# Five grad V stores of a decode attention backward, issued by GpSimd in pieces that leave out one DMA engine

## The chip, the cores and the metric

One core of one Trainium2 chip. The metric is the device time of one execution in microseconds (us). The engines are named as in the profile: PE (TensorE) does matmuls, PEld is its weight load, DVE is VectorE, ACT is ScalarE, POOL is GpSimd, SP is SyncE. ACT, SP and POOL can issue DMAs; the transfers themselves are done by 16 DMA engines that the core has.

## The reference

Attention with one query row per head, forward and backward. B, H, Sq, Sk, D = 2, 32, 1, 8192, 128, all in bfloat16, so there are 64 heads, each with a K and a V of 8192 x 128 (2 MB each).

```python
def _fwd_reference(q, k, v):
    scale = q.shape[-1] ** -0.5
    scores = jnp.einsum("bhqd,bhkd->bhqk", q, k) * scale
    p = _softmax(scores, axis=-1)
    return jnp.einsum("bhqk,bhkd->bhqd", p, v)
...
    _out, _vjp = jax.vjp(_f, q, k, v)
    _grads = _vjp(grad_out)
```

The outputs are the attention output, grad q (both 64 x 128), grad K and grad V (64 x 8192 x 128 each). In one head, with weights p: dp = V grad_out; ds = p (dp - sum(p dp)) scale; grad V is the outer product of p and grad_out, grad K that of ds and q. Some 268 MB are read and 268 MB written.

## The kernel before

A head's K lies in SBUF as 128 partitions of 64 rows of 128 numbers, 16 KB on each partition; V likewise. Five such pairs of buffers (kt, vt; UNITS = 5) are used in turn. K and V are loaded whole, one DMA each on SP's queue (load, L103). PE transposes 128 x 128 blocks with an identity (L112), ACT copies most of them and DVE a few from PSUM to bfloat16 (L119, L117), PE multiplies the transposed blocks with the columns of q and grad_out (L135), which gives scores and dp. Softmax runs on DVE and ACT (L159 to L227). PE then adds up the weighted rows for the output and grad q (L240). DVE writes the outer products over the inputs: grad V into the buffer of V, grad K into the buffer of K (outer, L270, in four quarters each), and `store` (L278) sends the buffer to HBM as one DMA of 128 x 16 KB on ACT's queue. The last head's stores go in halves.

The order is written out by hand. The loop runs over h; iteration h computes scores and dp of head h and finishes head p = h - 1 (weighted rows, outer products, stores), in NS = 8 steps j. The store of grad V of p stands in step 4, that of grad K in step 7, and at the end of step 7 SP is given the loads of head h + 3, which take the buffers of head h - 2 and therefore wait until its two stores have landed:

```python
                if x and p < BH - 1 and j in (4, 7):
                    store(p, j // 7)
...
                    for i in ((), (0,), (1, 2), (3, 4), (5,), (6,), (7,), ())[j]:
                        outer_and_store(p, i // 4, i % 4)
...
                    if x and UNITS <= h + 3 < BH:
                        load(h + 3)
```

The DMAs of SP and ACT carry eight semaphores in turn, so a DMA also waits until the eighth one before it has landed; in an iteration there are two stores and two loads, so a store waits for the same store two heads before. GpSimd makes the identities and fills the zero blocks of wz at the start (L292) and does nothing afterwards.

Of the kernel before, what the change touches and what calls it, by code (L numbers as in the profile page):

```python
# [11 lines left out]
BF16 = mybir.dt.bfloat16  # L12
# [3 lines left out]
HC = CH // 2  # L16
QG = 4
OG = 4
UNITS = 5


@with_exitstack
def kernel(
# [11 lines left out]
    nc = tc.nc  # L35
# [6 lines left out]
    assert NT * P == Sk and NT == 4 * CH and BH <= P and BH % QG == 0  # L42
    assert BH % OG == 0 and OG * 8 == 32
    NS = 2 * NT // CH
    scale = float(D) ** -0.5

    const = ctx.enter_context(tc.tile_pool(name="const", bufs=1))
# [6 lines left out]

    pick = const.tile([P, 4, 2, OG], F32)
    idv = ident_f[:].rearrange("p (g w k j) -> p g j w k", g=4, w=2, k=OG)
    nc.vector.tensor_copy(out=pick[:], in_=idv[:, 0])
    for g in range(1, 4):
        nc.vector.tensor_add(out=pick[:], in0=pick[:], in1=idv[:, g])

    q_rows = q.rearrange("b h s d -> (b h s) d")
# [3 lines left out]

    kvp = ctx.enter_context(tc.tile_pool(name="kv", bufs=UNITS))
    evp = ctx.enter_context(tc.tile_pool(name="ev", bufs=5))
# [8 lines left out]
    dk_v = out_2.rearrange("b h (p n) d -> (b h) p n d", n=NT)  # L76
    dv_v = out_3.rearrange("b h (p n) d -> (b h) p n d", n=NT)
# [8 lines left out]
    wz = [  # L86
        [const.tile([P, NT // 4, 32], BF16, name=f"wz{w}{k}") for k in range(OG)]
        for w in range(2)
# [5 lines left out]
    heads = [Head() for _ in range(BH)]  # L94

    def load(h):
        x = heads[h]
        x.kv = [
            kvp.tile([P, NT, D], BF16, name="kt", tag="kt"),
            kvp.tile([P, NT, D], BF16, name="vt", tag="vt"),  # L100
        ]
        for dst, src in zip(x.kv, (k_v, v_v)):
            nc.sync.dma_start(out=dst[:], in_=src[h])  # L103

    def transposes(h, j, u):

        x = heads[h]
        w, c = divmod(j, NS // 2)
        tp = ps_tp.tile([P, HC, P], F32, name="tp", tag="tp")
        for i in range(HC):  # L110
            n = c * CH + u * HC + i
            nc.tensor.matmul(  # L112
                tp[:, i, :], lhsT=x.kv[w][:, n, :], rhs=ident_bf[:], start=True, stop=True
            )
        ev = evp.tile([P, HC, P], BF16, name="ev", tag="ev")
        if u and j in (0, 7):
            nc.vector.tensor_copy(out=ev[:], in_=tp[:])  # L117
        else:
            nc.scalar.copy(out=ev[:], in_=tp[:])  # L119
        x.ev = getattr(x, "ev", {})  # L120
        x.ev[j, u] = ev

    def products(h, j, u):
        x = heads[h]
        w, c = divmod(j, NS // 2)
        if c == 0 and u == 0:
            if w:
                x.dp = ps_one.tile([P, NT + 2], F32, name="dp", tag="dp")
            else:
                x.sm = ps_one.tile([P, NT + P + 1], F32, name="sm", tag="sm")  # L130
        ev = x.ev.pop((j, u))
        col = (qT_all, doT_all)[w][:, h : h + 1]
        for i in range(HC):
            n = c * CH + u * HC + i
            nc.tensor.matmul(  # L135
                (x.dp if w else x.sm)[:, n : n + 1], lhsT=ev[:, i, :], rhs=col,
                start=True, stop=True,
            )
# [22 lines left out]
    def all_max(x):  # L161
        mT = x.sm[0:1, NT : NT + P]
        nc.tensor.transpose(mT, x.mp[:], ident_f[:])  # L163
        x.gm = work.tile([1, 1], F32, name="gm", tag="gm")
        nc.vector.reduce_max(out=x.gm[:], in_=mT, axis=AX.X)

    def exps(x):
        mb = x.sm[:, NT + P : NT + P + 1]
        nc.tensor.matmul(mb, lhsT=ones_f[0:1, :], rhs=x.gm[:], start=True, stop=True)  # L169
        negm = work.tile([P, 1], F32, name="negm", tag="negm")  # L170
        nc.vector.tensor_scalar(out=negm[:], in0=mb, scalar1=-scale, scalar2=None, op0=ALU.mult)  # L171
        x.E = work.tile([P, NT], F32, name="E_f", tag="E_f")
        x.ld = work.tile([P, 2], F32, name="ld", tag="ld")
        nc.scalar.activation(  # L174
            out=x.E[:],
            in_=x.sm[:, 0:NT],
            func=ACT.Exp,
            bias=negm[:],
            scale=scale,
            accum_out=x.ld[:, 0:1],  # L180
        )

    def to_weights(h, w, src):
        k = h % OG
        nc.vector.tensor_copy(  # L185
            out=wz[w][k][:, :, 16 * w + 4 * k : 16 * w + 4 * k + 4],
            in_=src[:].rearrange("p (m j) -> p m j", j=4),
        )

    def deltas(x):  # L190
        junk = work.tile([P, NT], BF16, name="junk", tag="junk")
        nc.vector.tensor_tensor_reduce(  # L192
            out=junk[:],
            in0=x.E[:],
            in1=x.dp[:, 0:NT],
            scale=1.0,
            scalar=0.0,
            op0=ALU.mult,
            op1=ALU.add,
            accum_out=x.ld[:, 1:2],  # L200
        )

    def sums(x):
        x.lsum = x.dp[:, NT : NT + 2]
        nc.tensor.matmul(x.lsum, lhsT=ones_f[:], rhs=x.ld[:], start=True, stop=True)  # L205
# [27 lines left out]
    def weighted_rows(h, w, chunks):  # L233


        rows, k = heads[h].kv[1 - w], h % OG
        for c in chunks:
            for g in range(4):
                n = c * CH + 4 * g
                nc.tensor.matmul(  # L240
                    acc[32 * g : 32 * g + 32, :],
                    lhsT=wz[w][k][:, n // 4, :],
                    rhs=rows[:, n : n + 4, :].rearrange("p n d -> p (n d)"),
                    start=(w == 0 and k == 0 and c == 0),
                    stop=(w == 1 and k == OG - 1 and c == NT // CH - 1),
                    tile_position=(0, 32 * g),
                )
# [17 lines left out]
    def outer(h, w, i):  # L265
# [8 lines left out]
            op=ALU.mult,  # L274
        )

    def store(h, w, a=0, b=NT):
        nc.scalar.dma_start(out=(dv_v, dk_v)[w][h][:, a:b, :], in_=heads[h].kv[1 - w][:, a:b, :])  # L278

    def outer_and_store(h, w, i):  # L280
# [3 lines left out]
            store(h, w, (i - 1) * CH, (i + 1) * CH)  # L284


    nat = const.tile([BH, 2, D], BF16)
    for i, src in enumerate((q_rows, do_rows)):
        nc.scalar.dma_start(out=nat[:, i, :], in_=src)
# [8 lines left out]
    with tc.manual_schedule():  # L298
        for h in range(min(UNITS, BH)):
            load(h)  # L300
        for h in range(BH + 1):
            p = h - 1
            x = heads[p] if h else None
            y = heads[h] if h < BH else None
            full = h and p % OG == OG - 1
            for j in range(NS):
                for u in range(2):
                    if y:
                        transposes(h, j, u)
                    if u == 0:  # L310
                        if x and j == 1:
                            sums(x)
                        if y and j == 5:
                            all_max(y)
                        if y and j == 6:
                            exps(y)
                    if y and j:
                        products(h, j - 1, u)
                    elif x and j == 0:
                        products(p, NS - 1, u)  # L320
                    if x and j < 4:
                        weighted_rows(p, j // 2, (2 * (j % 2) + u,))
                if x and j == 0:
                    deltas(x)
                if x and j == 1:
                    weights(p)
                if y and j == 4:
                    row_max(y)
                if y and j == 7:
                    to_weights(h, 0, y.E)  # L330
                if x and p < BH - 1 and j in (4, 7):
                    store(p, j // 7)
                if x:
                    for i in ((), (0,), (1, 2), (3, 4), (5,), (6,), (7,), ())[j]:
                        outer_and_store(p, i // 4, i % 4)
                    if full and j == 4:
                        acc_to_sbuf(x)
                    if full and j == 6:
                        combine(p)
                if j == 7:  # L340
                    if x and UNITS <= h + 3 < BH:
                        load(h + 3)
                    if y and h % QG == 0:
                        spread_rows(h // QG)
        for w, dst in enumerate((o_rows, dq_rows)):
            tps = ps_tp.tile([BH, P], BF16, name="tps", tag="tp")
            nc.tensor.transpose(tps[:], colsT[:, w, :], ident_bf[:])
            rows = const.tile([BH, D], BF16, name=f"rows{w}")
            nc.scalar.copy(out=rows[:], in_=tps[:])
            nc.scalar.dma_start(out=dst, in_=rows[:])  # L350


# [28 lines left out]
```

## Time and profile before

| | |
|---|---|
| median of 3 runs | 1305.08 us (1302.08 to 1305.24) |
| the profiled execution | 1302.89 us, its span 1301.1 us |
| mean granted TensorE clock | 0.885 |
| PE, PEld, DVE, ACT, POOL busy | 1108.2, 911.0, 887.4, 906.3, 4.8 us (85, 70, 68, 70, 0%) |
| moved by DMA | 539.65 MB in 37653 packets, mean 415 GB/s |
| loads, SP queue: issue to landing | K 18.9 us, V 28.5 us (median of 64 each) |
| stores, ACT queue: issue to landing | grad V 38.2 us, grad K 40.3 us (median of 63 each) |
| the longest group | L119 ACT, 896 copies of 1025 ns, 879.8 us |

The span is from the first to the last instruction of the profiled execution; the rest of its time lies around it. A share counts busy time over the whole span. "To landing" runs from the issue of a DMA to the arrival of its last bytes, with all that it waits for behind other transfers. A packet is what a DMA engine moves as one piece; here nearly all are one partition's 16 KB. Queue q1 carries the loads, q10 the stores and the small transfers of ACT, q8 the fetches of instructions.

### The profile page before, as it was taken

How to read it: one execution, taken by the hardware profiler on the slowest of the kernel's cores; microseconds unless marked ns; L12 is line 12 of the kernel's file. 1: busy time of each engine (PE TensorE's matmuls, PEld its weight loads, DVE VectorE, ACT ScalarE, POOL GpSimd, SP SyncE). 2: the span in 40 equal slices, each digit the busy share in tenths (PEclk: the TensorE clock that was granted, in tenths of full speed). 3: DMA queues.
4: the chain of work that ended last, by engine and by line, in shares of the span. 5: the costliest groups of instructions: out<-in, count | busy, mean ns of one | idle time of the engine just before them, and what ended most of it. 6: DMA issues, size and time to landing. Idle time of an engine off the chain costs nothing.

```text
span 1301.1 us, 42243 instructions
## 1 busy us (share of the span) xinstructions
PE 1108.2 (85%) x18948; PEld 911.0 (70%) x18948; DVE 887.4 (68%) x1511; ACT 906.3 (70%) x1043; POOL 4.8 (0%) x16
## 2 busy tenths in 40 slices
PE   5999998988889879898898888988889888888784
PEld 5777777766767667677776767767767677677673
DVE  2887777766766767667676676766667667676566
ACT  5887778867767767676776766766668576676562
POOL 1000000000000000000000000000000000000000
PEclk9999989889887998888898888888899888898786
DMA  9999999999999999999999999999999999999986
GB/s 396 418 427 427 426 428 426 428 427 429 427 428 426 426 419 421 421 427 421 418 421 421 426 421 418 421 408 421 416 418 417 411 425 419 413 412 421 391 356 268
DMA packets 37653, 539.65 MB, mean 415 GB/s; under 512 B 4448, under 2 KB 4448, under 8 KB 4448
## 3 DMA queue, kind: packets, MB, share of 16 engines
q1 hardware_dynamic: 18432, 268.44, 49.6%
q10 hardware_dynamic: 19040, 268.51, 48.7%
q8 instruction: 148, 2.42, 0.7%
q14 instruction: 33, 0.27, 0.1%
HBM read 268.47 MB, written 268.47 MB: 413 GB/s over the span
## 4 chain that ended last, share of the span: by engine, by line
DMA 76%; PE 10%; ACT 6%; issue 4%; DVE 3%; ACTq 0%; DVEq 0%; SPq 0%
DMA out_dram<-kt 74%; PE tp L112 6%; ACT ev L119 5%; DVE ev L117 2%; PE acc L240 2%; DMA kt<-in_k_dram 1%; PE sm L135 1%; DMA nat<-in_grad_out_dram 1%; PE dp L205 0%; DVE kt L270 0%; DVE vt L270 0%; PE dp L135 0%; ACT E_f L174 0%; PE c L258 0%; PE sm L163 0%
## 5 line engine op out<-in xcount | busy, mean ns | idle before, releaser
L119 ACT CAST ev<-tp 128x1024 bf16<-128x1024 f32 x896 | 879.8, 1025 | 326.7 <-PE tp L112 270.7
L112 PE MATMUL tp<-ident_bf,kt 128*128 128x128 bf16 x4096 | 375.8, 245 | 83.3 <-DMA kt<-in_k_dram 54.8
L112 PEld LDWEIGHTS <-kt 128*128 128x128 bf16 x4096 | 281.1, 110 | 218.0 <-issue 156.4
L112 PE MATMUL tp<-ident_bf,vt 128*128 128x128 bf16 x4096 | 316.7, 221 | 60.4 <-ACT ev L119 44.3
L135 PEld LDWEIGHTS <-ev 128*128 128x128 bf16 x8192 | 332.4, 100 | 2.1 <-issue 0.2
L112 PEld LDWEIGHTS <-vt 128*128 128x128 bf16 x4096 | 260.9, 98 | 94.6 <-issue 74.2
L117 DVE CAST ev<-tp 128x1024 bf16<-128x1024 f32 x128 | 156.7, 1224 | 246.0 <-PE tp L112 237.3
L270 DVE TENSOR_TENSOR kt<-qd,dS 128x2048 bf16<-128x2048 bf16 x256 | 310.0, 1212 | 0.0
L270 DVE TENSOR_TENSOR vt<-qd,P 128x2048 bf16<-128x2048 bf16 x256 | 295.8, 1216 | 0.0
L135 PE MATMUL dp<-doT_all,ev 128*128 128x1 bf16 x4096 | 178.9, 165 | 0.1
L135 PE MATMUL sm<-qT_all,ev 128*128 128x1 bf16 x4096 | 178.6, 164 | 0.0
L240 PE MATMUL acc<-vt,wz 128*32 128x512 bf16 x1024 | 124.3, 476 | 9.3 <-DVE wz L185 9.2
L240 PE MATMUL acc<-kt,wz 128*32 128x512 bf16 x1024 | 108.2, 415 | 0.4 <-DVE wz L185 0.4
L240 PEld LDWEIGHTS <-wz 128*32 128x32 bf16 x2048 | 53.6, 95 | 21.7 <-DVE wz L185 12.4
L159 DVE TENSOR_REDUCE mp<-sm 128x1 f32<-128x64 f32 x64 | 14.4, 225 | 74.3 <-PE sm L135 74.3
L153 ACT CAST qd<-pb 128x1024 bf16<-128x1024 f32 x16 | 16.2, 1012 | 43.4 <-DMA out_dram<-kt 39.6
L210 DVE RECIPROCAL rl_all<-dp 128x1 f32<-128x1 f32 x64 | 10.8, 168 | 39.6 <-PE dp L205 39.6
L205 PE MATMUL dp<-ld,ones_f 128*128 128x2 f32 x128 | 28.4, 291 | 8.8 <-DVE ld L192 8.6
L205 PEld LDWEIGHTS dp<-ld,ones_f 128*128 128x128 f32 x128 | 24.8, 242 | 14.1 <-DVE ld L192 13.5
L171 DVE TENSOR_SCALAR negm<-sm 128x1 f32<-128x1 f32 x64 | 9.9, 154 | 23.9 <-PE sm L169 23.9
L169 PE MATMUL sm<-gm,ones_f 1*128 1x1 f32 x128 | 24.4, 257 | 0.0
L169 PEld LDWEIGHTS sm<-gm,ones_f 1*128 1x128 f32 x128 | 18.9, 184 | 6.7 <-issue 0.2
(40 smaller groups left out, 277.4 us busy)
## 6 DMA issues: line engine op xcount, KB each, us to landing
kt<-in_k_dram SPq DMA_DIRECT2D x64, 2048.0 KB, 18.9
vt<-in_v_dram SPq DMA_DIRECT2D x64, 2048.0 KB, 28.5
out_dram<-vt ACTq DMA_DIRECT2D x63, 2048.0 KB, 38.2
out_dram<-kt ACTq DMA_DIRECT2D x63, 2048.0 KB, 40.3
out_dram<-vt ACTq DMA_DIRECT2D x2, 1024.0 KB, 8.4
out_dram<-kt ACTq DMA_DIRECT2D x2, 1024.0 KB, 8.5
out_dram<-rows ACTq DMA_DIRECT2D x2, 16.0 KB, 7.4
nat<-in_q_dram ACTq DMA_DIRECT2D x1, 16.0 KB, 8.2
```

The lines of the kernel that those rows point to most:

```text
L112: nc.tensor.matmul(tp[:, i, :], lhsT=x.kv[w][:, n, :], rhs=ident_bf[:], start=True, stop=True)
L117: nc.vector.tensor_copy(out=ev[:], in_=tp[:])
L119: nc.scalar.copy(out=ev[:], in_=tp[:])
L135: nc.tensor.matmul((x.dp if w else x.sm)[:, n : n + 1], lhsT=ev[:, i, :], rhs=col, start=True, stop=True,)
L153: nc.scalar.copy(out=qd[:], in_=pb[:])
L159: nc.vector.reduce_max(out=x.mp[:], in_=x.sm[:, 0:NT], axis=AX.X)
L169: nc.tensor.matmul(mb, lhsT=ones_f[0:1, :], rhs=x.gm[:], start=True, stop=True)
L171: nc.vector.tensor_scalar(out=negm[:], in0=mb, scalar1=-scale, scalar2=None, op0=ALU.mult)
L205: nc.tensor.matmul(x.lsum, lhsT=ones_f[:], rhs=x.ld[:], start=True, stop=True)
L210: nc.vector.reciprocal(out=rl, in_=x.lsum[:, 0:1])
L240: nc.tensor.matmul(acc[32 * g : 32 * g + 32, :], lhsT=wz[w][k][:, n // 4, :], rhs=rows[:, n : n + 4, :].rearrange("p n d -> p (n d)"), sta ...
L270: nc.vector.tensor_tensor(out=x.kv[1 - w][:, n : n + CH, :].rearrange("p n (d t) -> p n d t", t=2), in0=row.unsqueeze(1).to_broadcast([P, ...
```

## The change

Where (2h + w) mod 26 is 12, that is for grad V (w = 0) of heads 6, 19, 32, 45 and 58, `store` no longer issues one DMA on ACT's queue but calls `store_by_fifteen`, which issues the same 128 partitions from GpSimd in 24 pieces: for each r of 0 to 3, eleven partitions from 52 + r in steps of 4, four from r, three from 20 + r, eight from 96 + r and four from 32 + r, and the pair 16 + r and 48 + r (`fifth`). These pairs are the eight partitions that the change ascribes to the fifth DMA engine. The pieces of four are given 16384 as the longest run (`max_dma_last_dim`), the others 8192. Between the pieces stand ten small transfers, `turn(n)`, which copy four numbers of each of n rows of q into a scratch tile (`spare`), each into columns of its own; they are there to move the turn in which GpSimd's DMAs are given to engines. One more `turn(5)` stands at the start, ahead of the fills of wz on GpSimd, and a `turn(11)` at the end: 5 x 34 + 2 = 172 DMAs from GpSimd in all.

```diff
+RARE = 26
...
+    turns = []
+
+    def turn(n):
+
+        i = 4 * len(turns)
+        turns.append(n)
+        two = lambda t: t.rearrange("p (a b) -> p a b", a=2)
+        nc.gpsimd.dma_start(
+            out=two(spare[0:n, :])[:, :, i : i + 2], in_=two(q_rows[0:n, :])[:, :, 0:2]
+        )
+
+    def store_by_fifteen(h, w):
...
+        dst, src = (dv_v, dk_v)[w][h], heads[h].kv[1 - w]
+
+        def rows(lo, n, step=4, size=8192):
+            own = slice(lo, lo + step * (n - 1) + 1, step)
+            nc.gpsimd.dma_start(out=dst[own], in_=src[own], max_dma_last_dim=size)
+
+        def fifth(r):
+            rows(16 + r, 2, step=32)
+
+        for r in range(4):
+
+            if r == 1:
+                fifth(r)
+                turn(14)
+            rows(52 + r, 11)
+            rows(r, 4, size=16384)
+            if r == 0:
+                fifth(r)
+                turn(3)
+            elif r == 3:
+                turn(10)
+                fifth(r)
+                turn(9)
+            else:
+                turn(5)
+            rows(20 + r, 3)
+            if r == 2:
+                fifth(r)
+                turn(14)
+            rows(96 + r, 8)
+            rows(32 + r, 4, size=16384)
+            turn(5)
+
     def store(h, w, a=0, b=NT):
+        if (2 * h + w) % RARE == RARE // 2 - 1:
+            return store_by_fifteen(h, w)
         nc.scalar.dma_start(out=(dv_v, dk_v)[w][h][:, a:b, :], in_=heads[h].kv[1 - w][:, a:b, :])
...
+    spare = const.tile([16, 1024], BF16)
+    turn(5)
     nat = const.tile([BH, 2, D], BF16)
...
             nc.scalar.dma_start(out=dst, in_=rows[:])
+        turn(11)
```

## The prediction

> **What bounds the kernel now.** I read the page's strip and DMA parts first, then its chain, then the chain in order of time, then stretches of the span, and last the packet records behind them.
>
> The page:
>
> ```profile
> DMA  9999999999999999999999999999999999999986
> GB/s 396 418 427 427 426 428 426 428 427 429 427 428 426 426 419 421 421 427 421 418 421 421 426 421 418 421 408 421 416 418 417 411 425 419 413 412 421 391 356 268
> ...
> q1 hardware_dynamic: 18432, 268.44, 49.6%
> q10 hardware_dynamic: 19040, 268.51, 48.7%
> q8 instruction: 148, 2.42, 0.7%
> ...
> DMA 76%; PE 10%; ACT 6%; issue 4%; DVE 3%; ACTq 0%; DVEq 0%; SPq 0%
> ```
>
> The DMA engines are never idle, yet what they move sinks from 427 to some 415 GB/s: something takes longer per byte late in the run, with no engine seen idle. The chain is DMA. In order of time it repeats every four heads (columns: start, length, what):
>
> ```profile
> 1011.59 40.25 DMA out_dram<-kt
> 1051.90 37.05 DMA out_dram<-kt
> 1088.96 3.42 issue
> 1092.37 40.41 DMA out_dram<-kt
> 1132.85 36.71 DMA out_dram<-kt
> 1169.56 3.70 issue
> ```
>
> 40.4 + 36.7 + 3.7 = 80.8 us for four heads, 20.2 a head: a K store lands and lets the K store two heads later be issued (its semaphore is the one of eight DMAs before), and the loads into its buffer. SyncE shows the same; its waits in all:
>
> ```profile
> SPq L103 <- DMA out_dram<-kt: 1143.0, 59, 40.5
> ```
>
> Stretches of the span (busy us of PE, PEld, DVE, ACT and POOL, clock, DMA share, GB/s):
>
> ```profile
> 100.00:300.00 200.00, 180.37 (x3232) 148.37 (x3231) 150.29 (x257) 154.16 (x178) 0.00 (x0) 0.94 1.01 427
> 900.00:1100.00 200.00, 172.61 (x2935) 141.43 (x2934) 136.53 (x234) 139.91 (x162) 0.00 (x0) 0.88 1.00 417
> ...
> 1229.50:1233.00 3.50, 0.00 (x0) 0.00 (x0) 0.47 (x1) 0.00 (x0) 0.00 (x0) 1.00 0.35 150
> ...
> 1265.00:1272.50 7.50, 7.22 (x144) 5.92 (x141) 7.23 (x12) 6.54 (x7) 0.00 (x0) 1.00 0.11 42
> ```
>
> A DMA share of 0.11 is below two engines of 16, so in the tail nearly all others wait for one. To see whether that one is late all along, I followed the engines through the trace's packet records (start, length, queue, bytes). A 16 KB packet takes 611 ns and the next on its engine starts 4 ns before it ends; each 2 MB transfer gives every engine eight packets and a 4-byte one that counts it done. With these two rules the records fall into 16 rows up to 1139 us of the span:
> - One engine (the laggard) has packets of median 628 ns and up to 685; it finishes 1.580 packets per us throughout (1738 in 1100 us).
> - Eight engines have 611 ns packets and a gap of some 0.9 us about every 70 us, as long as the fetches on q8 (median 949 ns; 148 / 8 = 18.5 each): 1.612 per us before they are held back.
> - Seven have 611 ns and no such gaps: 1.64.
>
> So the laggard falls behind: by 4 packets at 139 us, 15 at 439, 26 at 839, and then no more, since the others wait for it. Late stores land on it 27 us after the others (store of V 47: others at 974, it at 1001). Each engine has the equal of 2048 packets: 65 are done at 39 us of the span, so the laggard needs 39 + 1983 / 1.580 = 1294 us, and the last large store ends at 1295 (some 6 us of small stores follow). The whole run is the length of this one engine's work. The profiled execution took 1302.89 (span 1301.1 and 1.8 around it), 2.2 below the median 1305.08 of the three runs; these took no profile and are as long, so the lag is no work of the profiler.
>
> **The change, part by part.**
>
> *Eight rows taken off one engine, five times.* 5 x 8 = 40 packets at 1 / 1.580 us are 25.3 us of the laggard's time, if the fifth engine is the laggard. It then ends at 39 + (2008 - 65) / 1.580 = 1269 of the span instead of 1294. The rows go one each to eight others: 5 x 0.61 = 3.1 us each. The fetch engines become its equals: 39 + 1983 / 1.612 = 1269, or 1272 for one that gets five rows more; the seven fast ones end at 1251. So the work bound falls by 22 to 25 us. A head costs 32 / 1.612 = 19.85 us against 20.2, or 422 GB/s against 414.
>
> *The tail.* It holds 13.5 us in which 15 engines wait: 3.5 at 1229.5, 7.5 at 1265, 2.5 at 1282.5. The first two are mostly the laggard (V of the last head lands on it at about 1261, on the others about 1255); the last is VectorE's products before the final stores. Balanced, some 5 us of idle time remain for every engine, where the laggard now has nearly none. That is given back: 1269 to 1272, plus 5, is 1274 to 1277 for the last large store, 18 to 21 us sooner.
>
> *Can compute follow at 19.85 us?* Up to 300 us it ran ahead: V stores 5, 8 and 11 are issued 54.7 and 51.7 us apart, 17.2 to 18.2 a head. PE has 1108 / 64 = 17.3 us of work a head. Yes, with some 1.5 us to spare.
>
> *34 DMAs on GpSimd in place of one on ScalarE* (24 pieces, 10 small transfers), five times, 172 with the two at the ends. GpSimd works only in the first 5.4 us, so nothing queues behind them but the eight fills of wz at the start, first needed after the first loads. The one before them on the queue is the first small transfer. What counts is when all 24 pieces have landed, since the V buffer waits for that. No row shows a DMA issued by GpSimd. Lower bound: 0.34 us each, as one on ScalarE's queue: 34 x 0.34 = 12 us. Upper bound: each waits for the one before to land, and the shortest landing of a store is 7.0: 34 x 7.0 = 238 us. With waits eight back, as the loads and stores have them, it is 34 / 8 x 7.0 = 30 us and a last landing, 37. I take 37, as these rows are the nearest. The whole store takes 38.2 today. The Trainium skill (DMA: Bandwidth & Descriptors, § Specifications) gives about 1 us to the first byte of a DMA from GpSimd; one after the other, 34 would be some 34 us, an estimate, and the sum would stay as it is. The same skill (SBUF — State Buffer, § SBUF: two separate sides) warns that VectorE instructions in a two-port mode keep GpSimd from writing descriptors, which speaks against this change; no row here shows it.
>
> What covers 37 us: the K store of the same head lands 10 us after the V store, and SyncE asks for the K buffer first, so 48 us cost nothing. Beyond, the load queue runs dry, but four stores in flight are 32 packets, 19 us more of work. So up to some 68 us the engines stay busy; beyond, each us is lost. ScalarE's next stores meet their old semaphores earlier or as now, since one DMA fewer lies between.
>
> *Packets.* An 8 KB packet takes 309 ns (the last stores' row), twice that is 7 ns over 611: 16 to 18 on an engine, 0.1 us a store. Small transfers: some 150 runs of 4 bytes, 9 an engine, between 9 ns (the counting packet) and 18 (a 256-byte one): 0.2 us. 34 counting packets on each engine: 34 x 6 to 9 ns = 0.3 us. Together 0.6 us a store, 3 us in all. Below nothing is excluded: it is work added.
>
> *Sum:* 1302.9 - 20 + 3 = 1286; on the median 1305.1 - 17 = 1288. I say 1287.
>
> **Rivals.**
> - *The laggard isn't the fifth engine, or the pieces fall on other engines than meant.* The trace gives packets no engine number, so nothing in it says which of the 16 is late. The laggard keeps its 1294 us, and at worst takes five more rows (3 us) and the 3 us of small packets: 1303 to 1309, no change. Chance 0.10. The Trainium skill (DMA: Bandwidth & Descriptors, § Latency and other measured facts) has engines 7 and 15 as the usually slower ones, and by that the change would unload the wrong engine; the trace disagrees so far, with one slow engine and not two. The skill also says (same page, § Why a DMA increments its semaphore by 16 and not by 1) that a DMA from GpSimd takes k consecutive engines from a round-robin cursor: by that the pieces pass by engine 4, which has rows 16 to 19 and 48 to 51 (§ The descriptor swizzle), only if the cursor starts at 0.
> - *Half of it.* Nine engines are then within 3 us of each other, and a transfer ends with its slowest; if the backlog evens that out badly at 0.15 us a head, 9 us are lost: 1296. For it: 15 engines have slower packets when little is queued (417 against 427 GB/s). Against: 26 packets of play. Chance 0.14.
> - *Slower: the small transfers, all into one tile, wait for each other to land.* Ten waits of 7.0 and 24 issues of 0.34 make 78 us a store, 10 past the 68 that are covered; five times, 50 us: 1287 + 50 = 1337. It decides from about 72 us a store (4 us past the cover, five times, eat the gain), 2.1 us a DMA. Longer waits make it far worse. For it: 34 DMAs in a row, with no row for their price. Against: their columns in the tile are disjoint. Chance 0.16.
>
> **How the numbers follow.** Forecast 0.60 (1280 to 1293 by itself: 25 us off and nothing given back, to 10 us more given back), half 0.14, nothing 0.10, slower 0.16. A measurement of this kernel tells some 0.3%, 3.9 us, from no change: faster is below 1301, slower above 1309. So 0.74, 0.10, 0.16. The range runs from 1280 to 1309: it leaves out the slower case and a little below.
>
> **What would show it.** Right: GB/s of some 422 to the end; the chain's K stores under 40 us at a pace of 19.85 a head; the stretches of DMA share 0.35 and 0.11 in the tail gone or short; one engine's packets still 628 ns, but never over 10 packets behind; GpSimd's pieces landed within 48 us of the first. Wrong: the laggard still 26 behind at 900 us; a wait of SyncE on a GpSimd store of over 30 us beyond its usual; slices in the GB/s strip far below 400 at heads 6, 19, 32, 45 and 58.

## The result and the profile after

The changed kernel takes 1286.99 us (median of 4 runs, 1286.19 to 1287.69) against 1305.16 for the kernel before (1302.08 to 1305.4): a ratio of 0.9866, 95% interval 0.9849 to 0.9883. The profiled execution took 1286.92, its span 1285.1. The forecast was 1287.0.

The page of the changed kernel, the lines that answer to those shown of before:

```profile
DMA  9999999999999999999999999999999999999998
GB/s 396 418 426 428 426 426 425 423 431 427 426 426 426 413 424 427 423 427 425 428 426 399 427 426 418 428 427 428 419 403 426 425 419 391 428 429 425 425 424 336
...
q1 hardware_dynamic: 18432, 268.44, 49.5%
q10 hardware_dynamic: 18320, 258.02, 47.4%
q0 software_dynamic: 6944, 10.51, 2.2%
...
PE 40%; DMA 26%; ACT 19%; DVE 11%; issue 3%; ACTq 0%; DVEq 0%; SPq 0%
...
out_dram<-vt POOLq DMA_DIRECT2D x20, 176.0 KB, 23.2
```

Before, the strip sank from 427 to some 415 GB/s and stayed there; now it keeps returning to about 425 up to the last slice but one, with short dips (399, 403, 391). The new queue q0 holds what GpSimd issues. The chain is no longer DMA: its 76% have become 26%. The last line is the surprise: a piece of 176 KB lands 23 us after its issue.

The stretches of the span, in the columns shown before, with those of the tail:

```profile
100.00:300.00 200.00, 162.91 (x2994) 134.66 (x2993) 137.91 (x235) 142.83 (x164) 19.95 (x35) 0.94 1.01 426
900.00:1100.00 200.00, 162.66 (x2790) 135.92 (x2787) 129.35 (x219) 135.48 (x156) 19.88 (x35) 0.85 1.00 415
...
1250.00:1262.00 12.00, 10.21 (x189) 8.23 (x185) 8.43 (x16) 8.57 (x11) 3.92 (x7) 0.95 1.01 422
1262.00:1272.00 10.00, 4.00 (x32) 2.03 (x24) 9.96 (x15) 0.00 (x0) 0.00 (x0) 0.50 0.98 410
```

The stretches from 900 to 1100 are hardly apart (415 GB/s after, 417 before): two of those dips lie in them. The holes of the tail are gone: no stretch of DMA share 0.35 or 0.11 is left before the last stores run out. By the packet records the mean idle time of an engine in the last 60 us before the end of the last large packet is 5.0 us, where it was 13.7 (instruction fetches count as idle).

The same records show that the pieces went where they were meant to go. In each of the first two stores (heads 6 and 19) the engine with the long packets (median 632 ns) got no data packet at all; in the first, seven engines got eight rows and eight got nine. Counting the 16 rows that it was spared, the laggard is level with the others at 450 us (703 + 16 against a median of 719.5 packets); before the change it was 15 behind at 439 us. Later in the run two of the rows that I follow cross, and I don't read them engine by engine.

### The profile page after: what moved, and what is told of

Its sections match the earlier page's. It is cut to its first block, busy times and chain, and to the rows that moved or that the text cites. A ratio compares the mean times of both kernels' runs of the same rounds, so it can differ in the third digit from the quotient of the medians.

```text
span 1285.1 us, 42433 instructions
## 1 busy us (share of the span) xinstructions
PE 1060.3 (83%) x18948; PEld 877.3 (68%) x18948; DVE 883.8 (69%) x1511; ACT 909.3 (71%) x1043; POOL 105.8 (8%) x193
## 4 chain that ended last, share of the span: by engine, by line
PE 40%; DMA 26%; ACT 19%; DVE 11%; issue 3%; ACTq 0%; DVEq 0%; SPq 0%
PE tp L113 23%; ACT ev L120 18%; DMA vt<-in_v_dram 9%; DVE ev L118 9%; DMA out_dram<-vt 9%; PE acc L241 9%; DMA kt<-in_k_dram 4%; PE sm L136 4%; DMA out_dram<-kt 3%; PE dp L206 1%; PE dp L136 1%; PE c L259 1%; DMA nat<-in_grad_out_dram 1%; ACT E_f L175 1%; PE sm L170 1%
## 5 line engine op out<-in xcount | busy, mean ns | idle before, releaser
L113 PE MATMUL tp<-ident_bf,vt 128*128 128x128 bf16 x4096 | 327.4, 225 | 134.7 <-ACT ev L120 121.6
L113 PEld LDWEIGHTS <-vt 128*128 128x128 bf16 x4096 | 268.9, 100 | 167.3 <-issue 153.2
L113 PE MATMUL tp<-ident_bf,kt 128*128 128x128 bf16 x4096 | 335.9, 228 | 17.2 <-DMA kt<-in_k_dram 6.5
L113 PEld LDWEIGHTS <-kt 128*128 128x128 bf16 x4096 | 249.4, 101 | 131.5 <-issue 123.2
L136 PEld LDWEIGHTS <-ev 128*128 128x128 bf16 x8192 | 324.4, 98 | 2.2 <-issue 0.2
L299 POOL DMA_DIRECT2D out_dram<-vt x120 | 67.0, 560 | 1032.7 <-DVE vt L271 832.1
L241 PE MATMUL acc<-vt,wz 128*32 128x512 bf16 x1024 | 109.3, 418 | 17.8 <-DVE wz L186 17.8
L241 PE MATMUL acc<-kt,wz 128*32 128x512 bf16 x1024 | 103.4, 396 | 0.1
L285 POOL DMA_DIRECT2D spare<-in_q_dram x57 | 34.1, 598 | 121.1 <-DMA out_dram<-vt 107.0
L206 PEld LDWEIGHTS dp<-ld,ones_f 128*128 128x128 f32 x128 | 20.6, 202 | 31.1 <-DVE ld L193 31.0
L211 DVE RECIPROCAL rl_all<-dp 128x1 f32<-128x1 f32 x64 | 10.7, 168 | 32.0 <-PE dp L206 32.0
```

The costliest lines, as they stand in the source:

```text
L113: nc.tensor.matmul(tp[:, i, :], lhsT=x.kv[w][:, n, :], rhs=ident_bf[:], start=True, stop=True)
L136: nc.tensor.matmul((x.dp if w else x.sm)[:, n : n + 1], lhsT=ev[:, i, :], rhs=col, start=True, stop=True,)
L241: nc.tensor.matmul(acc[32 * g : 32 * g + 32, :], lhsT=wz[w][k][:, n // 4, :], rhs=rows[:, n : n + 4, :].rearrange("p n d -> p (n d)"), sta ...
L285: nc.gpsimd.dma_start(out=two(spare[0:n, :])[:, :, i : i + 2], in_=two(q_rows[0:n, :])[:, :, 0:2])
L299: nc.gpsimd.dma_start(out=dst[own], in_=src[own], max_dma_last_dim=size)
```

## The experiments

All times are medians; each ratio is to the kernel before, run beside it, with its 95% interval. The kernel before had medians of 1302.5 to 1305.2 us in these sessions, so a difference between times of two sessions is good to some 3 us.

**One engine earlier: the cleanest test.** One number is changed at the start and its counterpart at the end:

```diff
-    turn(5)
+    turn(4)
...
-        turn(11)
+        turn(12)
```

> The changed kernel with one number changed: the first small transfer has 4 rows instead of 5 (and the last 12 instead of 11), so that every cut piece falls one engine earlier. The fifth engine then gets its eight rows and one more, and the sixteenth is left out but for one row. Number, kinds and times of the DMAs are the same. Theory: the laggard has 5 rows more than before the change, 1303 to 1309. Rival (the gain is in how the stores are issued, not in which engine they leave out): 1287.

1320.72 us, ratio 1.0144 (1.0119 to 1.0170). In the packet records of its first store the engine with the 636 ns packets has nine rows, and another one has a single row. The same DMAs in the same order, with another engine left out, are 34 us slower than the changed kernel (36 by the two ratios): the gain is in *which* engine is left out. But it isn't 1303 to 1309: it is 12 us slower than that, so the way the stores are issued costs something that I had not counted.

**Stores whole from GpSimd.** `store_by_fifteen` issues one DMA, and there are no small transfers:

```diff
         dst, src = (dv_v, dk_v)[w][h], heads[h].kv[1 - w]
-        for r in range(4):
...
+        nc.gpsimd.dma_start(out=dst, in_=src)
```

> The five stores are issued by GpSimd as one DMA each of 128 partitions over all 16 engines, no pieces and no small transfers. Theory: the laggard keeps all its rows, 1302 to 1308, no change from before. Rival 1 (the gain is that ScalarE has five stores fewer to wait with): about 1287.

1318.44, ratio 1.0096 (1.0076 to 1.0116): neither. Moving five of 126 stores to GpSimd *costs* 14 us when the laggard keeps its rows. The stores themselves land 19.9 us after their issue (median), sooner than those on ScalarE's queue before the change (38.2). ScalarE's waits for DMAs, the kernel before and this one (us in total, times, longest):

```profile
ACT qd L153 <- DMA out_dram<-kt: 39.6, 12, 3.8
ACT ev L119 <- DMA out_dram<-kt: 16.7, 5, 4.2
```

```profile
ACT ev L120 <- DMA vt<-in_v_dram: 69.6, 5, 16.2
```

Before, ScalarE waits briefly, at a store, for the same store of two heads before. Now it stands five times for up to 16 us, waiting for the load of a V. The semaphores that the DMAs carry in the traces show how: with one DMA less on the two queues, the eight no longer go round in step, and a V store comes after a load on its semaphore (5 V stores before the change, 14 in this kernel, 23 in the changed kernel). The last of these waits falls into the tail of the whole-store kernel (in the stretches, the last two columns are DMA share and GB/s):

```profile
1267.00:1275.00 8.00, 7.65 (x146) 6.11 (x147) 7.22 (x16) 6.89 (x7) 0.00 (x0) 1.00 0.24 97
...
1283.00:1293.00 10.00, 9.33 (x178) 7.37 (x176) 9.04 (x17) 7.60 (x8) 0.00 (x0) 1.00 0.27 113
```

There PE is busy nearly all the time and most DMA engines stand idle. By the packet records one engine with long packets works on alone from 1270 to 1275; then there are stretches in which no engine moves a packet of a load or a store: 0.4 us at 1275.4, 5.7 at 1287.4, 1.1 at 1304.4. The kernel before and the changed kernel have no such stretch.

**Is it the tail?** The same with the store of head 58 back on ScalarE's queue:

```diff
-        if (2 * h + w) % RARE == RARE // 2 - 1:
+        if h < 58 and (2 * h + w) % RARE == RARE // 2 - 1:
```

> Whole stores from GpSimd as in the run that came out at 1318, but only at heads 6, 19, 32 and 45: the one near the end (head 58) goes back to ScalarE's queue. Theory T (the 13 us are lost in the tail: ScalarE stands 16 us for a V load after head 58's store, and with five heads left nothing queued makes that good, while after the other four the laggard stays busy): 1302 to 1307. Rival (each such store costs the same, 2.7 us): 1313.

1309.16, ratio 1.0043 (1.0029 to 1.0057), between the two. Leaving out one store of five takes away 9 us by the medians and 7 by the ratios, and no stretch without packets is left in the tail, so the one near the end is by far the dearest; the other four still cost some 1.6 us each (6.5 / 4).

**Is it the waits for semaphores?** A small copy on ScalarE's queue stands in for each missing store, to keep the eight in step:

```diff
+            nc.scalar.dma_start(out=fill[:, i : i + 4], in_=q_rows[0:16, 0:4])
             return store_by_fifteen(h, w)
```

> The five stores whole from GpSimd, as in the run that came out at 1318, plus a small copy on ScalarE's queue in the place of each of them, so that the turn of the eight semaphores stays as before the change. Theory S (the 13 us lost there are ScalarE waiting at a V store for a V load that had the semaphore before it, 70 us of waits): 1302 to 1308. Rival (the third queue itself disturbs the other two): 1318.

> The changed kernel plus such a small copy on ScalarE's queue in place of each of the five stores. In the changed kernel ScalarE waits 64 us for V loads at stores that follow them on a semaphore; with the turn kept, these waits go. Theory S: the engines' work still sets the end (1269 to 1272 of the span and some 5 us of tail), so 1282 to 1286, 1 to 5 us faster than the changed kernel. Rival (these waits lie beside the DMA engines' work and cost nothing): 1287.

Whole stores with the copies: 1313.15, ratio 1.0074 (1.0055 to 1.0093), where 1.0096 (1.0076 to 1.0116) was measured without them: the intervals overlap. The changed kernel with the copies: 1295.49, ratio 0.9936 (0.9920 to 0.9952), 8.5 us *slower* than without. Theory S falls in both. With whole stores the copies did restore the turn (5 V stores behind a load, as before the change), and the trace has no wait of ScalarE for a DMA at all; yet the kernel takes 10.7 us more than the kernel before. In the second kernel the copies didn't restore it (again 23 V stores behind a load): ScalarE waits for V loads ten times, 101.5 us in all, where the changed kernel has four such waits, 63.9. Its middle is as well filled as that of the changed kernel, but one wait falls into the last 94 us:

```profile
ACT ev L120 <- DMA vt<-in_v_dram: 16.8, 1, 16.8
```

and in its tail the engines stand:

```profile
1260.00:1270.00 10.00, 9.32 (x175) 7.37 (x172) 9.22 (x17) 8.03 (x9) 0.00 (x0) 1.00 0.29 120
```

The stretches in which no engine moves a packet of a load or a store come to 7.1 us in the whole-store kernel, 6.8 in the second kernel with copies and 4.0 in the first, all in the tail. So a wait of ScalarE near the end is dear: the second kernel lost 8.5 us, and it has 6.8 us of such standstill where the changed kernel has none. In the middle of the changed kernel it is nearly free: from the start of each of its four waits for a V load to 25 us after it, an engine stands idle for 1.5 us at most, on average. In the whole-store kernel that is up to 4.6 us.

This isn't the whole of the 14 us. With whole stores and copies some 7 us are lost beside the standstill, without any wait of ScalarE for a DMA, and the rival that the third queue itself disturbs the other two still stands. One sign of it is in the traces: in both whole-store kernels the first store from GpSimd overtakes the K store issued 12 us before it. That K store lands at 167 and 168 us, where it landed at 161 before the change, and the K load that waits for it goes out 6 to 7 us later. Whether that makes up the rest isn't shown.

**The small transfers alone.** All stores whole on ScalarE's queue, the `turn` calls kept:

```diff
         def rows(lo, n, step=4, size=8192):
...
-            nc.gpsimd.dma_start(out=dst[own], in_=src[own], max_dma_last_dim=size)
+            return
...
-            return store_by_fifteen(h, w)
+            store_by_fifteen(h, w)
```

> The kernel before plus the 57 small transfers alone; all stores whole on ScalarE's queue. They cost what they add: 3 us of packets by the prediction at most, so 1304 to 1309. If they cost more than 4 us, the changed kernel's gain would be larger without them.

1306.92, ratio 1.0018 (1.0001 to 1.0034): between 0 and 4 us by the interval, as expected.

**How many stores.** Two (heads 19 and 45), and, in the same way, ten (heads 3, 9, ... 57):

```diff
-        if (2 * h + w) % RARE == RARE // 2 - 1:
+        if w == 0 and h in (19, 45):
```

> As the changed kernel with two such stores (heads 19 and 45) in place of five. Theory: the laggard is 16 packets shorter, 16 / 1.580 = 10 us: 1294 to 1297. Rival (one engine's lag is a threshold effect, or the gain comes from something else that one store already gives): 1287 or 1305.

1298.16, ratio 0.9961 (0.9948 to 0.9974), a gain of 3 to 7 us where 10 were worked out.

> As the changed kernel with ten such stores, one in six heads. Theory: the laggard ends 25 us sooner still, but the fetch engines set the end and some of them carry ten rows more: no gain over five, 1286 to 1292, of it 3 us packets of the small transfers. Rival (the gain goes on with the number of stores): about 1268. With stores of 100 us on GpSimd every 120 us, the V buffers are short by one most of the time; if that costs, 1300 and more.

1292.89, ratio 0.9921 (0.9898 to 0.9944). No gain over five but a loss of 6: that fits a laggard that is already level, so that more rows off it bring nothing and each further store has its price.

**Three kernels that missed their aim.** A new `store_by_fifteen` sent the pairs uncut, without small transfers around them, and passed by the engine with the number SKIP:

```diff
+            rows(32 + 4 * (SKIP + 1) + r, 15 - SKIP)
+            rows(r, SKIP, size=16384)
+            rows(4 * SKIP + r, 2, step=32, size=16384)
+            turn(SKIP + 1)
```

> As the changed kernel, but the eight rows of the fifth engine go uncut, which should put all of them on the first two engines (20 rows more on each, 12 us, on engines that end 18 us before the fetch engines) and none on a fetch engine; 32 DMAs a store instead of 35. Theory (the laggard's work set the end, now the fetch engines' does): 1283 to 1287. Rival 1 (the gain comes from taking stores off ScalarE's queue, whatever engines they use): 1287. Rival 2 (evenness over many engines matters, two engines with 20 rows more become late): 1290 to 1300.

> The same code with one number changed: the pieces pass by the sixth engine instead of the fifth. Theory: the laggard keeps its eight rows five times, so 1303 to 1309, as before the change. Rival 1 (off ScalarE's queue) and any reason that is not about the fifth engine: about 1287.

> The same code, passing by the eighth engine. Theory: 1303 to 1309. Rival (the slow engine is the one that the notes name, the eighth): 1283 to 1290, and the kernel that passes by the fifth would then owe its gain to something else.

1305.73, 1331.44 and 1328.01; ratios 1.0013 (1.0003 to 1.0024), 1.0198 (1.0180 to 1.0215), 1.0177 (1.0160 to 1.0193). The packet records show why they tell nothing of which engine is slow: the pieces didn't fall where they were meant to, probably because the uncut pairs moved the turn. In the first store the engines got 3 to 16 rows in the first two kernels and 1 to 16 in the third, the laggard 4, 12 and 12. Seen so, they are of use: by the laggard's rows in the first store the kernels with five stores from GpSimd, but for those with copies or with named buffers, stand in order, 0 rows 1287, 4 rows 1306, 8 (whole) 1318, 9 (one engine earlier) 1321, 12 rows 1328 and 1331. From 0 to 12 that is 41 to 44 us, 3.4 to 3.7 a row; one row five times at 0.633 us is 3.2. The other four stores of these kernels weren't followed, and other engines got up to 16 rows in them, so this is a rough scale.

**Where a store of 100 us hides.** GpSimd's first store in the changed kernel, then what SyncE issues meanwhile (start, length, engine and line, operation):

```profile
144.27 1.68 POOL L299 DMA_DIRECT2D out_dram<-vt  x3 [138.04 <-DVE vt L271]
...
148.18 0.62 POOL L285 DMA_DIRECT2D spare<-in_q_dram  x1
154.41 0.56 POOL L299 DMA_DIRECT2D out_dram<-vt  x1 [5.61 <-DMA out_dram<-vt]
...
229.88 0.61 POOL L285 DMA_DIRECT2D spare<-in_q_dram  x1 [3.70 <-DMA out_dram<-vt]
```

```profile
171.40 0.33 SPq L104 DMA_DIRECT2D kt<-in_k_dram  x1
181.69 0.33 SPq L104 DMA_DIRECT2D vt<-in_v_dram  x1
...
256.51 0.33 SPq L104 DMA_DIRECT2D kt<-in_k_dram  x1
266.13 0.33 SPq L104 DMA_DIRECT2D vt<-in_v_dram  x1
275.94 0.33 SPq L104 DMA_DIRECT2D kt<-in_k_dram  x1
276.55 0.79 SPq L104 DMA_DIRECT2D vt<-in_v_dram  x1
```

After eight DMAs in a row GpSimd waits for each to land before the eighth after it, and the last data packet of the store ends at 244.2. Yet V of head 11, five heads later, is loaded at 181.69: it can't be in the buffer of head 6. Five V loads come some 10 us behind their K, and at 276.55 the two go together again: each took the buffer of the head after the one it would have taken. The slow buffer, last in the row, was taken at 276.55, 132 us after the store's begin (the load waits there for a semaphore of GpSimd's DMAs). An experiment ties the buffers to the head:

```diff
-            kvp.tile([P, NT, D], BF16, name="vt", tag="vt"),
+            kvp.tile([P, NT, D], BF16, name=f"vt{h % UNITS}", tag=f"vt{h % UNITS}", bufs=1),
```

(and K's likewise).

> As the changed kernel, but each head is given its buffers by name (head modulo 5), so that the buffer of a V that GpSimd stores can't be handed to a later head than the fifth after it. In the changed kernel such a store takes 100 us, and the V load five heads later starts 37 us after the store's begin, in another buffer; the buffer of the slow store is taken 122 us after its begin. Theory H (this handing on hides the 100 us): the V load of five heads later now waits until 100 us, some 52 us past the 48 at which it would come anyway, of which 19 us are covered by queued stores: 33 us five times, about 1450. Rival (the 100 us would be hidden anyway): 1287.

1312.50, ratio 1.0072 (1.0050 to 1.0094), 25.5 us above the changed kernel: handing on the buffer is worth 5 us a store, a sixth of what I expected and not nothing. SyncE's queue shows the V load of head 11 standing until the store is done, 48 us after K:

```profile
171.46 0.33 SPq L104 DMA_DIRECT2D kt<-in_k_dram  x1
219.97 0.33 SPq L104 DMA_DIRECT2D vt<-in_v_dram  x1
220.46 0.33 SPq L104 DMA_DIRECT2D kt<-in_k_dram  x1
```

PE then waits 45.2 us for V loads in five waits, and the mean idle time of an engine grows from 13 to 31 us between 50 us and the last 60 us, and from 5 to 12 in these: together nearly the whole of the 25.5. One reason why it is less than I expected shows in the records: with the loads held back the store is done sooner, its data packets running from 148.6 to 219.2 (to 244.2 in the changed kernel).

## Why the prediction was right, and where it wasn't

*What bounds the kernel* was right. The end was set by one engine with long packets; it is the one that the change leaves out (no row on it), and the same DMAs with another engine left out don't gain. By the Trainium skill (DMA: Bandwidth & Descriptors, § Latency and other measured facts) engines 7 and 15 are the usual slow ones; the runs show one slow engine. The placement agrees with the same page's account of the engines that GpSimd's DMAs take in turn (§ Why a DMA increments its semaphore by 16 and not by 1), as the rows per engine show.

*The size* was right in the sum, by two terms that were both too small. The rows off the laggard were put at 25 us less 5 given back. Between the two kernels that differ in one number they are worth 34 (45 rows instead of 40, at 0.633 us 28.5; the rest isn't taken apart, but the holes are fewer). Against that, issuing from GpSimd was put at 3 us and costs 14 without pieces, 18 with them and five rows more on the laggard. 18 - 34 is -16 and 3 - 20 was -17; measured were -18 (the kernel before had 1305.2 beside the changed kernel, and 1302.5 beside the one with another engine left out). The forecast's number was therefore partly luck. Its bound for the work (1269 to 1272 of the span) isn't measured by itself: the last large packet ends at 1283.1, 11 to 14 us later, where the prediction had left 8 (5 of tail, 3 of packets). It had also read the end before the change too early: by the packet records one engine has large packets up to 1299.3, not 1295, and from there to 1283.1 it is 16.

*Ten small transfers and 34 DMAs* were a slip in counting: there are eleven a store, so 35 and, with the two at the ends, 177. Nothing turns on it.

*The landing of a piece* failed. I took 7.0 us, the shortest landing of a store, a row of the tail with little queued; in the middle of the run a piece waits its turn on full engines and lands after 23. GpSimd then issues no faster than its pieces land. With 35 DMAs and eight in flight that is 35 / 8 x 23 = 100 us, as measured, and not 37. The bounds had it (12 to 238), the value was taken from the wrong row. So the sign that the pieces land within 48 us of the first didn't come, and the forecast survived it only because of the next point.

*The cover* of 48 and 68 us failed too: it supposed that a buffer goes to the head five later. A store of 100 us would by my rule have cost (100 - 68) x 5 = 160 us. The buffer was handed to the head ten later, 132 us after the store's begin, and even with tied buffers the price is 25.5 us. That the 100 us cost so little was luck: nothing in the prediction provided for it.

*"ScalarE's next stores meet their old semaphores earlier or as now"* failed: they meet those of loads, and wait 63.9 us in four waits. In the middle of the run, where all four lie, that left the engines idle for 1.5 us a wait at most.

*The tail* was right in kind: 13.7 us of idle time an engine became 5.0, the 5 that the prediction left.

Of the rivals, the wrong engine is refuted by the rows per engine, *half of it* (1296) didn't come, and the waits of small transfers for each other are there in another form (eight in flight) without the price. Of the signs, the rate of some 422 GB/s to the end came only in part (415 from 900 to 1100 us, 424 to 426 from 1200 to 1250).

## What to carry to other kernels

When all DMA engines look busy and the rate still sinks, follow the engines one by one through the packet records: a kernel whose transfers all use every engine alike runs at the pace of the slowest, and a few rows taken off that one shorten the run until it is level with the others. What is moved to another queue has side prices that no busy row shows: which semaphore the next DMAs wait on, and which buffer is handed to whom; look at the waits of every queue, and keep such a step away from the end of the run, where little is queued that could make a wait good. Take a duration from a row of the same load: a landing time from an idle tail says nothing of full engines.

## What the runs showed of the hardware that I had not expected

- One of the 16 DMA engines is 3 to 4% slower on 16 KB packets (median 628 to 637 ns against 611) in every run in which I could follow it, and on both chips that the experiments ran on (7 and 9) it is the engine on which the pieces of the change put no row. Unlike eight others it shows none of the 0.9 us gaps that go with instruction fetches.
- A DMA issue occupies GpSimd for 0.56 to 0.60 us; ScalarE's and SyncE's take 0.33 to 0.34.
- Pieces of four rows in uncut 16 KB runs fell on the same four engines in the first store (8 uncut packets each) and left the turn where it was, as the rows of the other pieces show; the spread of the kernels with uncut pairs suggests that those moved it.
